# Remainder chunk thresholded by a parametric ReLU on ScalarE, with gMLP jobs, transfers and weight chores in another order

## The chip, the core and the metric

The kernel runs on one core of a Trainium2 chip. The metric is the device time of one execution in microseconds (us). Of the kernel before, three executions took 562.84, 564.09 and 565.11 us; their median is 564.09 us.

## The reference

Thresholded attention over 8 batches of 8 heads (576 positions, 64 dimensions per head) is followed by a gMLP block with a spatial gate. Cut to what matters:

```python
scores = scale * q @ k.T                       # per batch and head, 576 x 576
scores = where(scores >= max(scores) - tau, scores, -1e9)
attn   = exp(scores - max(scores)); attn /= sum(attn)
x      = attn @ v                              # heads side by side: 576 x 512 per batch
h      = relu(x @ w_in); u, v = h[:, :512], h[:, 512:]
v_n    = (v - mean(v)) / sqrt(var(v) + 1e-6)   # over the 512 features of a position
v_s    = w_spatial @ v_n + b_spatial           # over positions, 576 x 576
out    = (u * v_s) @ w_out
```

## The kernel before

**Slots and steps.** Two heads make a pair, and the 32 pairs (four to a batch) are worked through one after another; the time of one pair is a *slot*. A slot has five *steps*, c = 0 to 4, and the running number of a step is g = 5 x slot + c. Steps 0 to 3 take 128 query rows of both heads (a chunk of 128 x 1152 scores). Step 4 is the *remainder chunk*: the last 64 rows of both heads, stacked on 128 partitions (128 x 576).

**What a step does**, in the order in which `step` (L478) writes it into the engines' queues: TensorE multiplies the scores into PSUM (`scores`, L448 and L445); evictions that were held from the step before are done (`held`); the first filler job `f1` runs its products and, if it is of the kind "act", its eviction on ScalarE; VectorE takes the negated row maxima (`negm`, L491); an `f1` of the kind "dve" is evicted on VectorE; ScalarE computes `e = exp(s - max)` (L499); `mask` (L459) runs for the *previous* step's chunk; actions that have become due (`later`) run; and the second filler `f2` runs its products, evicted at once if it is "dve", or in the next step if it is "act". Every engine works its queue off in this order, and so does SyncE's DMA queue (SP), which issues nearly all transfers. [...]

**Mask.** For steps 0 to 3 VectorE computes `p = (e >= exp(-tau)) * e` in bf16 (L464), and after every second step one DMA transpose brings two chunks into `pT` (L468). For the remainder it computes `pr` the same way (L473), and a small transpose makes `ptr` (L476). Because `mask` works for the previous step, `pr` and `ptr` of a slot are written into the queues in step 0 of the next.

**Fillers.** Steps 0 to 2 transpose q and k of the next pair on TensorE (`qk_main`, `qk_rem`); steps 3 and 4 multiply the previous pair's weights by v (`pv`, L266), each ending in a reciprocal `r` (L274) and a product `xn` (L275) on VectorE. When both heads of a pair are done, a DMA transpose writes their part of `xT` (L281). From g = 27 on, each step also has one gMLP job of a finished batch: five `v` jobs (`moe_v`, gate branch), five `u` (`moe_u`), five `s` (`moe_s`, spatial products) and five `o` (`moe_o`, output). The string `ORDER` (L527) sets which job takes which of the batch's 20 steps. If a step has two fillers, those of kind "act" come first.

**The gate branch.** A `v` job's product is evicted by a ReLU with a row sum (`vrel`, L333); POOL makes `nmean` (L335). Through `later.append((1, rest))` one step passes, and then `rest` squares on ScalarE with a row sum (`sq`, L341) and normalizes on POOL in four instructions (L343, L345, L346, L347) into one of the five chunks of `vn`. Every `s` job reads all five chunks (L389).

**Transfers of results.** The transposes into `xT` and the stores of `o` are put into the list `sends`, and `step` issues them after the mask of the same step or, where the eviction came later than that, of the next step. Loads of q, k and v come from a queue that gives up one DMA per step.

**Start, weights, end.** The first loads of q and k go out on two queues (SP and ScalarE's); clearing of buffers is split between POOL (`clear_first`, `clear_rest`) and VectorE; eight transposes of `identf` run on TensorE ahead of the first real ones (L559). The weight *chores* (`load_w_in`, `load_ws`, `shape_ws`, `shape_bias`, `place_bias`, `load_w_o`) hang on certain steps (L519 to L522). After the last scores the list `last` is worked off two jobs at a time; there `moe_v_part` does three quarters of the last batch's `v` products before the last `xT` part has come.

Of the kernel before, what the change touches and what calls it, by code (L numbers as in the profile page):

```python
# [17 lines left out]
def kernel(  # L18
# [38 lines left out]

    identf = const.tile([P, P], F32, name="identf")
    ntau = const.tile([P, 1], F32, name="ntau")
    ctau = const.tile([P, 1], F32, name="ctau")  # L60

    mhalf = const.tile([P, 1], F32, name="mhalf")

    p_ring = [const.tile([P, 2, 1152], BF16, name=f"p{i}") for i in range(2)]
# [3 lines left out]
    ld_ring = [[const.tile([P, 4, 5, D], F32, name=f"{n}{i}") for n in ("ql", "kl", "vl")]  # L68
               for i in range(2)]
    vx_ring = [const.tile([P, 2, D], F32, name=f"vx{i}") for i in range(2)]  # L70
    kd_ring = [const.tile([P, P], F32, name=f"kd{i}") for i in range(2)]
    ptr_ring = [const.tile([P, 5, 192], BF16, name=f"ptr{i}") for i in range(3)]

    def clear_first():
        for t in ld_ring[0][:2]:
            nc.gpsimd.memset(t[64:128, :, 4, :], 0.0)
        nc.gpsimd.memset(kd_ring[0], 0.0)

    def clear_rest():
        nc.gpsimd.memset(ld_ring[0][2][64:128, :, 4, :], 0.0)  # L80
        nc.gpsimd.memset(kd_ring[1], 0.0)
        for t in vx_ring:
            nc.gpsimd.memset(t[0:64], 0.0)
        for t in ld_ring[1]:
            nc.gpsimd.memset(t[64:128, :, 4, :], 0.0)
        for t in v_ring:
            nc.vector.memset(t[:, :, D:D + 1], 1.0)
            nc.vector.memset(t[64:128, 4, D:D + 1], 0.0)
            nc.vector.memset(t[64:128, 9, D:D + 1], 0.0)
            nc.vector.memset(t[0:64, 10, D:D + 1], 0.0)  # L90
        for t in ptr_ring:
            nc.vector.memset(t[:, :, 128:192], 1.0)
        for t in pr_ring:
            nc.vector.memset(t[:, S:640], 0.0)
        for t in vn_ring:
            nc.vector.memset(t[64:128, 4, :], 1.0)

# [5 lines left out]

    def load(i, n, w, eng=nc.sync):

        b, hp = divmod(i, HP)
        t = ld_ring[i // 2 % 2][w][:, 2 * (i % 2):2 * (i % 2) + 2 * n]
        src = (q, k, v)[w][b, 2 * hp:2 * hp + 2 * n]

        def main():  # L110
            eng.dma_start(
                out=t[:, :, 0:4, :],
                in_=src[:, 0:512, :].rearrange("h (p c) d -> p h (c d)", c=4))

        def rest():
            eng.dma_start(out=t[0:64, :, 4, :],
                          in_=src[:, 512:576, :].rearrange("h p d -> p h d"))

        def rest_b():
            nc.sync.dma_start(  # L120
                out=vx_ring[i // 2 % 2][64:128],
                in_=src.rearrange("(j h) s d -> h s j d", h=2)[1, 512:576])
        return [main, rest] + ([rest_b] if w == 2 else [])
# [67 lines left out]
    def shape_bias(_):  # L191
# [6 lines left out]
        nc.gpsimd.tensor_copy(out=parts[:, 2, :], in_=b32)  # L198

    def place_bias(_):  # L200
        for n in range(3):
            nc.sync.dma_start(out=wsT[64 + n:65 + n, 4, 0:S], in_=parts[:, n, :])
# [11 lines left out]
    done_with = set()  # L214
    sends = []
    qks, pts, xns, xts = {}, {}, {}, {}
# [34 lines left out]
    def pv(i, h):  # L251
# [17 lines left out]
        def ev():  # L269
            o = hold["t"][:, 0:325].rearrange("p (c d) -> p c d", d=65)  # L270
            if h == 0:
                xns[i] = xp.tile([P, 5, P], BF16, name="xn")
            r = small.tile([P, 5], F32, name="r")
            nc.vector.reciprocal(out=r, in_=o[:, :, 64])  # L274
            nc.vector.tensor_tensor(out=xns[i][:, :, h * D:(h + 1) * D], in0=o[:, :, 0:64],  # L275
                                    in1=r.unsqueeze(2).broadcast_to([P, 5, 64]), op=ALU.mult)
            if h == 1:
                if hp == 0:
                    xts[b] = xtp.tile([P, 4, 640], BF16, name="xT")
                xn = xns[i]  # L280
                sends.append(lambda: nc.sync.dma_start_transpose(  # L281
                    out=xts[b][:, hp, :].rearrange("p (c s) -> p c s", s=P),
                    in_=xn.rearrange("p c d -> p (c d)")))
        return "dve", mm, ev
# [3 lines left out]

    parted = {}

    def moe_v_part(b, c):

        def mm():
            if c % 3 == 0:
                parted["tile"] = ps_s.tile([P, 1536], F32, name="s")
            t = parted[c] = parted["tile"][:, 512 * (c % 3):512 * (c % 3) + 512]
            for f in range(3):
                nc.tensor.matmul(out=t, lhsT=xts[b][:, f, c * P:(c + 1) * P],
                                 rhs=w_in[:, f, 512:1024], start=(f == 0), stop=False)
        return "act", mm, lambda: None  # L300

    def moe_v(b, c):
        hold = {}

        def mm():
            t = hold["t"] = parted.get(c) if b == B - 1 else bank()
            for f in range(3 if b == B - 1 else 0, 4):
                nc.tensor.matmul(out=t, lhsT=xts[b][:, f, c * P:(c + 1) * P],  # L308
                                 rhs=w_in[:, f, 512:1024], start=(f == 0), stop=(f == 3))
# [101 lines left out]
    def moe_o(b, c):  # L411
# [9 lines left out]
        def ev():  # L421
# [3 lines left out]
            else:  # L425
                nc.scalar.copy(out=o[:n], in_=hold["t"][:n])  # L426
            dst = (out[b, 0:512, :].rearrange("(p c) n -> p c n", c=4)[:, c, :] if c < 4
                   else out[b, 512:576, :])
            sends.append(lambda: nc.sync.dma_start(out=dst, in_=o[:n]))
        return "act", mm, ev  # L430
# [28 lines left out]
    def mask():  # L459
# [11 lines left out]
        else:  # L471
            pt = pr_ring[i % 2]
            nc.vector.scalar_tensor_tensor(out=pt[:, 0:S], in0=e[:, 0, :], scalar=ctau,  # L473
                                           in1=e[:, 0, :], op0=ALU.is_ge, op1=ALU.mult)
            pts[i, 2] = ptr_ring[i % 3]
            nc.sync.dma_start_transpose(out=pts[i, 2][:, :, 0:P], in_=pt)  # L476

    def step(i, c, f1, f2):  # L478
# [17 lines left out]
        if i is not None:  # L496
            e = ep.tile([P, 2, S], F32, name="e")
            for h in range(nh):
                nc.scalar.activation(out=e[:, h, :], in_=s[:, h, :], func=ACT.Exp,  # L499
                                     bias=nm[:, h:h + 1])  # L500
        ready = sends[:]
        sends.clear()
        if unmasked:
            mask()
        for f in ready:
            f()
        if i is not None:
# [10 lines left out]

    chores = {13: (load_bias, 0)}  # L519
    for n, g0, d, f in ((4, 6, 4, load_w_in), (3, 8, 4, load_ws), (5, 23, 3, shape_ws),  # L520
                        (1, 15, 1, shape_bias), (1, 37, 1, place_bias), (2, 42, 5, load_w_o)):
        chores.update({g0 + d * j: (f, j) for j in range(n)})  # L522
# [3 lines left out]
    LAG = 27  # L526
    ORDER = "vuvvuvuvuu" + "oososososs"  # L527
    jobs = {}
    for b in range(B - 1):
        n = dict.fromkeys("vuso", 0)  # L530
        for j, t in enumerate(ORDER):
            f = {"v": moe_v, "u": moe_u, "s": moe_s, "o": moe_o}[t]
            if t != "o" or b:
                jobs[LAG + 20 * b + j] = (f, b - (t == "o"), n[t])
            n[t] += 1
    last = [jobs.pop(g) for g in range(5 * NPAIR, LAG + 20 * B) if g in jobs]
    Z = B - 1
    last += [(moe_o, Z - 1, j) for j in (0, 1)]
    last += [(pv, NPAIR - 1, h) for h in range(2)]
    last += [(moe_v_part, Z, j) for j in range(5)]  # L540
    last += [(moe_v, Z, j) for j in range(5)]
    last += [(moe_o, Z - 1, j) for j in (2, 3, 4)]
    last += [(f, Z, j) for f in (moe_u, moe_s, moe_o) for j in range(5)]
    with tc.manual_schedule():
        for w in (0, 1):
            for f in load(0, 1, w, (nc.sync, nc.scalar)[w]):
                f()
        clear_first()
        make_identity(nc, identf)
        nc.vector.memset(ntau, -float(tau))  # L550
        nc.vector.memset(mhalf, -0.5)
        nc.scalar.activation(out=ctau, in_=ntau, func=ACT.Exp)
        for w in (0, 1):
            for f in load(1, 1, w):
                f()
        for f in load(0, 2, 2):
            f()
        for _ in range(8):
            nc.tensor.transpose(out=ps_f.tile([P, 512], F32, name="f")[:, 0:P], in_=identf,  # L559
                                identity=identf)  # L560
        shape_qk(0)
        for f in (qk_main(0, 0), qk_main(0, 1), qk_rem(0)):
            f[1]()
            f[2]()
        clear_rest()
        shape_qk(1)
        queue = []
        for g in range(5 * NPAIR + (len(last) + 1) // 2):
# [28 lines left out]
        while held:  # L597
            held.pop(0)()
        for f in sends:
            f()  # L600

# [34 lines left out]
```

## Time and profile before

| | |
|---|---|
| Three executions, median | 564.09 us (562.84 to 565.11) |
| The profiled execution's own time | 562.84 us |
| Its span, first to last instruction | 561.1 us |
| TensorE (PE) busy | 487.0 us, 87% |
| VectorE (DVE) busy | 470.5 us, 84% |
| ScalarE (ACT) busy | 328.2 us, 59% |
| GpSimd (POOL) busy | 240.8 us, 43% |
| Mean granted TensorE clock | 0.959 of full speed |

The first negated maximum starts at 12.5 us and the last at 518.6 us, so there are some 12 us of start, 506 us for 32 slots and 43 us of end; a slot takes 15.8 us on average. In the profile a group's line gives line, engine, operation, tiles, shape and count, then busy time, the mean of one in ns, and the idle time of the engine just ahead of it with what ended most of it. A timeline gives start, duration and the instruction; "PE", "DVE", "ACT", "POOL" and "SPq" are TensorE, VectorE, ScalarE, GpSimd and SyncE's DMA queue.

### The profile page before, as it was taken

The numbers are of one execution on the slowest core, as the hardware profiler recorded it, in microseconds if no ns is written. First come the engines' busy times: TensorE is split into PE (matmuls) and PEld (weight loads), VectorE is DVE, ScalarE is ACT, GpSimd is POOL, SyncE is SP. The second block draws the span as 40 slices with busy tenths as digits, with TensorE's granted clock in tenths as the row PEclk, the third lists the DMA queues.
The fourth block names the chain that finished last, engine by engine and source line by source line (L and its number), as shares of the span: only waits on it lengthen the run. The fifth ranks groups of instructions, "written<-read, shape, count | busy, mean of one in ns | idle before, by whom it ended". The sixth has DMA issues, their size and how long they took to land.

```text
span 561.1 us, 10240 instructions
## 1 busy us (share of the span) xinstructions
PE 487.0 (87%) x3848; PEld 257.7 (46%) x3848; DVE 470.5 (84%) x535; ACT 328.2 (59%) x609; POOL 240.8 (43%) x413
## 2 busy tenths in 40 slices
PE   6774887987898999899879999889989999989886
PEld 4342443544354555455435554445444554545433
DVE  3894988997898899889968999889987899989553
ACT  2553454774467755676546765677555766677241
POOL 5426622685407732377204752178303762064020
PEclk9896888997999999999999999999998999999989
DMA  8599797985987888968997698978987588755822
GB/s 235 107 214 185 140 207 134 217 146 125 208 173 158 180 182 184 195 94 224 166 174 145 127 217 150 189 141 165 205 187 157 98 198 188 119 107 102 192 65 84
DMA packets 243601, 90.91 MB, mean 162 GB/s; under 512 B 213024, under 2 KB 238112, under 8 KB 243552
## 3 DMA queue, kind: packets, MB, share of 16 engines
q1 hardware_dynamic: 241936, 88.39, 76.9%
q0 software_dynamic: 1200, 1.58, 2.3%
q8 instruction: 30, 0.49, 0.4%
q10 hardware_dynamic: 416, 0.30, 0.2%
q14 instruction: 19, 0.16, 0.1%
HBM read 33.31 MB, written 9.44 MB: 76 GB/s over the span
## 4 chain that ended last, share of the span: by engine, by line
PE 47%; DVE 24%; DMA 12%; ACT 10%; issue 5%; SPq 1%; POOL 0%; ACTq 0%; POOLq 0%
PE s L445 18%; DVE negm L491 14%; PE f L266 7%; DVE p L464 7%; DMA ptr<-pr 7%; ACT e L499 5%; PE f L389 4%; DMA xT<-xn 4%; PE s L448 3%; PE f L359 3%; PE f L308 3%; PE f L418 3%; ACT sq L341 2%; DVE xn L275 1%; ACT vrel L333 1%
## 5 line engine op out<-in xcount | busy, mean ns | idle before, releaser
L499 ACT ACTIVATE e<-s,negm 128x576 f32<-128x576 f32 x288 | 199.5, 740 | 96.8 <-DVE negm L491 77.4
L491 DVE TENSOR_REDUCE negm<-s 128x2 f32<-128x1152 f32 (+1 forms) x160 | 197.2, 1233 | 47.3 <-PE s L445 45.9
L445 PE MATMUL s<-qkT 64*128 64x512 f32 (+1 forms) x768 | 191.1, 590 | 1.0 <-ACT e L499 1.0
L464 DVE SCALAR_TENSOR_TENSOR p<-e,ctau 128x1152 bf16<-128x1152 f32 x128 | 187.5, 1465 | 0.0
L445 PEld LDWEIGHTS s<-qkT 64*128 64x128 f32 (+1 forms) x768 | 55.6, 173 | 29.2 <-issue 2.8
L247 POOL COPY kd<-qkT 64x64 f32<-64x64 f32 x32 | 13.0, 406 | 129.4 <-ACT qkT L243 124.7
L230 ACT COPY qkT<-f 128x512 f32<-128x512 f32 x64 | 37.6, 588 | 50.1 <-PE f L226 50.1
L266 PEld LDWEIGHTS <-pT 128*128 128x128 bf16 x1280 | 49.1, 100 | 37.4 <-issue 25.8
L448 PE MATMUL s<-kd,qkT 128*128 128x128 f32 x256 | 55.4, 299 | 8.5 <-ACT e L499 5.5
L266 PE MATMUL f<-v,pT 128*128 128x65 bf16 x1260 | 53.1, 197 | 9.0 <-ACT vrel L333 4.6
L448 PEld LDWEIGHTS s<-kd,qkT 128*128 128x128 f32 x256 | 45.5, 197 | 21.8 <-ACT e L499 8.8
L308 PE MATMUL f<-w_in,xT 128*128 128x512 bf16 x140 | 37.8, 387 | 11.0 <-DMA xT<-xn 9.5
L142 POOL COPY kn<-kl 128x640 f32<-128x640 f32 x32 | 26.1, 817 | 32.8 <-DMA kl<-in_k_dram 20.3
L389 PE MATMUL f<-wsT,vn 128*128 128x512 bf16 x150 | 38.0, 384 | 2.1 <-ACT o L426 1.6
L335 POOL TENSOR_SCALAR nmean<-sm 128x1 f32<-128x1 f32 x35 | 11.8, 338 | 64.8 <-ACT vrel L333 64.8
L266 PE MATMUL f<-v,ptr 128*128 128x65 bf16 x315 | 21.2, 199 | 19.2 <-DMA ptr<-pr 19.2
L359 PE MATMUL f<-xT,w_in 128*128 128x512 bf16 x120 | 32.6, 396 | 5.8 <-ACT vrel L333 5.8
L139 POOL TENSOR_SCALAR qn<-ql 128x640 f32<-128x640 f32 x32 | 30.5, 953 | 11.6 <-DMA ql<-in_q_dram 10.7
L418 PE MATMUL f<-w_o,gT 128*128 128x512 bf16 (+1 forms) x128 | 33.8, 388 | 0.5
L333 ACT ACTIVATE vrel<-f 128x512 f32<-128x512 f32 x35 | 20.8, 595 | 20.8 <-PE f L308 20.8
L275 DVE TENSOR_TENSOR xn<-f,r 128x320 bf16<-128x320 f32 x63 | 31.0, 491 | 2.2
L473 DVE SCALAR_TENSOR_TENSOR pr<-e,ctau 128x576 bf16<-128x576 f32 x32 | 31.9, 997 | 0.0
(101 smaller groups left out, 530.5 us busy)
## 6 DMA issues: line engine op xcount, KB each, us to landing
vl<-in_v_dram SPq DMA_DIRECT2D x16, 512.0 KB, 4.7
out_dram<-o SPq DMA_DIRECT2D x32, 256.0 KB, 2.7
ql<-in_q_dram SPq DMA_DIRECT2D x15, 512.0 KB, 4.5
kl<-in_k_dram SPq DMA_DIRECT2D x15, 512.0 KB, 4.6
uT<-in_moe_w_spatial_dram SPq DMA_DIRECT2D x2, 576.0 KB, 5.1
vl<-in_v_dram SPq DMA_DIRECT2D x16, 64.0 KB, 2.8
pT<-p SPq DMA_TRANSPOSE x64, 5.5
w_in<-in_moe_w_in_dram POOLq DMA_DIRECT2D x4, 256.0 KB, 5.7
```

The source lines that it names most:

```text
L230: nc.scalar.copy(out=qks[i][:, which, 0:512], in_=hold["t"])
L266: nc.tensor.matmul(out=t[:, c * 65:c * 65 + 65], lhsT=lhs, rhs=rhs, start=(j == 0), stop=(j == 4))
L275: nc.vector.tensor_tensor(out=xns[i][:, :, h * D:(h + 1) * D], in0=o[:, :, 0:64], in1=r.unsqueeze(2).broadcast_to([P, 5, 64]), op=ALU.mult)
L308: nc.tensor.matmul(out=t, lhsT=xts[b][:, f, c * P:(c + 1) * P], rhs=w_in[:, f, 512:1024], start=(f == 0), stop=(f == 3))
L359: nc.tensor.matmul(out=t, lhsT=w_in[:, m, f * P:(f + 1) * P], rhs=xts[b][:, m, 0:512], start=(m == 0), stop=(m == 3))
L389: nc.tensor.matmul(out=t, lhsT=vn[:, c, f * P:(f + 1) * P], rhs=wsT[:, c, 0:512], start=(c == 0), stop=(c == 4))
L418: nc.tensor.matmul(out=t[:n], lhsT=gs[b][:, f, c * P:c * P + n], rhs=w_o[:, f, :], start=(f == 0), stop=(f == 3))
L445: return nc.tensor.matmul(out=out, lhsT=qk[hs, 0, m], rhs=qk[hs, 1, lo:lo + n], start=True, stop=True)
L448: nc.tensor.matmul(out=view(s, 512, [[448, 2], [1, 64]]), lhsT=qk[:, 0, c * P:(c + 1) * P], rhs=kd_ring[i % 2], start=True, stop=True)
L464: nc.vector.scalar_tensor_tensor(out=pt[:, c % 2, :], in0=ef, scalar=ctau, in1=ef, op0=ALU.is_ge, op1=ALU.mult)
L491: nc.vector.tensor_reduce(out=nm[:, 0:nh], in_=s, axis=AX.X, op=ALU.max, negate=True)
L499: nc.scalar.activation(out=e[:, h, :], in_=s[:, h, :], func=ACT.Exp, bias=nm[:, h:h + 1])
```

## The change

The remainder chunk's threshold moves from VectorE to ScalarE: tau is added to the negated maximum (a 128 x 1 instruction on VectorE), a parametric ReLU with slope 1e30 below zero leaves values at or over the threshold and makes the others hugely negative, and an exp writes straight into `pr` in bf16. All values kept come out larger by exp(tau), which the division by the row sum cancels. Only the transpose into `ptr` stays in `mask`. In the same change the gMLP jobs alternate v, u and then s, o; `sends` is gone, so `xT` transposes and stores are issued where their eviction is written; `moe_v_part` is gone and `last` has another order; the weight chores hang on other steps, and `place_bias` is part of `shape_bias` again; all clearing is done on POOL ahead of the first loads; the first k load goes out on SP; and the eight transposes of `identf` are gone.

```diff
     identf = const.tile([P, P], F32, name="identf")
+    make_identity(nc, identf)
     ntau = const.tile([P, 1], F32, name="ntau")
+    nc.vector.memset(ntau, -float(tau))
...
+    for ts in ld_ring:
+        for t in ts:
+            nc.gpsimd.memset(t[64:128, :, 4, :], 0.0)
+    for t in vx_ring:
+        nc.gpsimd.memset(t[0:64], 0.0)
+    for t in kd_ring:
+        nc.gpsimd.memset(t, 0.0)
+    for t in v_ring:
+        nc.gpsimd.memset(t[:, :, D:D + 1], 1.0)
+        nc.gpsimd.memset(t[64:128, 4, D:D + 1], 0.0)
+        nc.gpsimd.memset(t[64:128, 9, D:D + 1], 0.0)
+        nc.gpsimd.memset(t[0:64, 10, D:D + 1], 0.0)
-    def clear_first():
...
-    def clear_rest():
...
+    for t in ptr_ring:
+        nc.gpsimd.memset(t[:, :, 128:192], 1.0)
+    for t in pr_ring:
+        nc.gpsimd.memset(t[:, S:640], 0.0)
+    for t in vn_ring:
+        nc.gpsimd.memset(t[64:128, 4, :], 1.0)
...
-
-    def place_bias(_):
         for n in range(3):
             nc.sync.dma_start(out=wsT[64 + n:65 + n, 4, 0:S], in_=parts[:, n, :])
...
-                xn = xns[i]
-                sends.append(lambda: nc.sync.dma_start_transpose(
+                nc.sync.dma_start_transpose(
                     out=xts[b][:, hp, :].rearrange("p (c s) -> p c s", s=P),
-                    in_=xn.rearrange("p c d -> p (c d)")))
+                    in_=xns[i].rearrange("p c d -> p (c d)"))
...
-    def moe_v_part(b, c):
...
-            t = hold["t"] = parted.get(c) if b == B - 1 else bank()
-            for f in range(3 if b == B - 1 else 0, 4):
+            t = hold["t"] = bank()
+            for f in range(4):
...
-            sends.append(lambda: nc.sync.dma_start(out=dst, in_=o[:n]))
+            nc.sync.dma_start(out=dst, in_=o[:n])
...
         else:
-            pt = pr_ring[i % 2]
-            nc.vector.scalar_tensor_tensor(out=pt[:, 0:S], in0=e[:, 0, :], scalar=ctau,
-                                           in1=e[:, 0, :], op0=ALU.is_ge, op1=ALU.mult)
             pts[i, 2] = ptr_ring[i % 3]
-            nc.sync.dma_start_transpose(out=pts[i, 2][:, :, 0:P], in_=pt)
+            nc.sync.dma_start_transpose(out=pts[i, 2][:, :, 0:P], in_=pr_ring[i % 2])
...
             e = ep.tile([P, 2, S], F32, name="e")
-            for h in range(nh):
+            if c == 4:
+
+                nc.vector.tensor_scalar_add(out=nm[:, 0:1], in0=nm[:, 0:1], scalar1=float(tau))
+                nc.scalar.activation(out=e[:, 0, :], in_=s[:, 0, :], func=ACT.Prelu,
+                                     bias=nm[:, 0:1], alpha=1e30)
+                nc.scalar.activation(out=pr_ring[i % 2][:, 0:S], in_=e[:, 0, :], func=ACT.Exp)
+            for h in range(2 if c < 4 else 0):
                 nc.scalar.activation(out=e[:, h, :], in_=s[:, h, :], func=ACT.Exp,
                                      bias=nm[:, h:h + 1])
-        ready = sends[:]
-        sends.clear()
         if unmasked:
             mask()
-        for f in ready:
-            f()
...
-    chores = {13: (load_bias, 0)}
-    for n, g0, d, f in ((4, 6, 4, load_w_in), (3, 8, 4, load_ws), (5, 23, 3, shape_ws),
-                        (1, 15, 1, shape_bias), (1, 37, 1, place_bias), (2, 42, 5, load_w_o)):
+    chores = {2: (load_bias, 0)}
+    for n, g0, d, f in ((4, 5, 2, load_w_in), (3, 12, 1, load_ws), (5, 16, 1, shape_ws),
+                        (1, 21, 1, shape_bias), (2, 23, 2, load_w_o)):
         chores.update({g0 + d * j: (f, j) for j in range(n)})
...
     LAG = 27
-    ORDER = "vuvvuvuvuu" + "oososososs"
     jobs = {}
     for b in range(B - 1):
-        n = dict.fromkeys("vuso", 0)
-        for j, t in enumerate(ORDER):
-            f = {"v": moe_v, "u": moe_u, "s": moe_s, "o": moe_o}[t]
-            if t != "o" or b:
-                jobs[LAG + 20 * b + j] = (f, b - (t == "o"), n[t])
-            n[t] += 1
+        for j in range(5):
+            g = LAG + 20 * b + 2 * j
+            jobs[g], jobs[g + 1] = (moe_v, b, j), (moe_u, b, j)
+            jobs[g + 10] = (moe_s, b, j)
+            if b:
+                jobs[g + 11] = (moe_o, b - 1, j)
     last = [jobs.pop(g) for g in range(5 * NPAIR, LAG + 20 * B) if g in jobs]
-    Z = B - 1
-    last += [(moe_o, Z - 1, j) for j in (0, 1)]
-    last += [(pv, NPAIR - 1, h) for h in range(2)]
-    last += [(moe_v_part, Z, j) for j in range(5)]
-    last += [(moe_v, Z, j) for j in range(5)]
-    last += [(moe_o, Z - 1, j) for j in (2, 3, 4)]
-    last += [(f, Z, j) for f in (moe_u, moe_s, moe_o) for j in range(5)]
+    last += [(moe_o, B - 2, j) for j in range(5)]
+    last[6:6] = [(pv, NPAIR - 1, h) for h in range(2)]
+    last += [(f, B - 1, j) for f in (moe_v, moe_u, moe_s, moe_o) for j in range(5)]
     with tc.manual_schedule():
         for w in (0, 1):
-            for f in load(0, 1, w, (nc.sync, nc.scalar)[w]):
+            for f in load(0, 1, w):
                 f()
-        clear_first()
...
-        for _ in range(8):
-            nc.tensor.transpose(out=ps_f.tile([P, 512], F32, name="f")[:, 0:P], in_=identf,
-                                identity=identf)
         shape_qk(0)
         for f in (qk_main(0, 0), qk_main(0, 1), qk_rem(0)):
             f[1]()
             f[2]()
-        clear_rest()
+        for w in (0, 1):
+            for f in load(1, 1, w):
+                f()
         shape_qk(1)
+        for f in load(0, 2, 2):
+            f()
```

More of the change, by code (lines that the diff above doesn't have):

```diff
@@ L58 @@
     identf = const.tile([P, P], F32, name="identf")
+    make_identity(nc, identf)
     ntau = const.tile([P, 1], F32, name="ntau")
+    nc.vector.memset(ntau, -float(tau))
     ctau = const.tile([P, 1], F32, name="ctau")
+    nc.scalar.activation(out=ctau, in_=ntau, func=ACT.Exp)
     mhalf = const.tile([P, 1], F32, name="mhalf")
+    nc.vector.memset(mhalf, -0.5)
     p_ring = [const.tile([P, 2, 1152], BF16, name=f"p{i}") for i in range(2)]
@@ L69 @@
                for i in range(2)]
+    for ts in ld_ring:
+        for t in ts:
+            nc.gpsimd.memset(t[64:128, :, 4, :], 0.0)
     vx_ring = [const.tile([P, 2, D], F32, name=f"vx{i}") for i in range(2)]
+    for t in vx_ring:
+        nc.gpsimd.memset(t[0:64], 0.0)
     kd_ring = [const.tile([P, P], F32, name=f"kd{i}") for i in range(2)]
-    ptr_ring = [const.tile([P, 5, 192], BF16, name=f"ptr{i}") for i in range(3)]
-    def clear_first():
-        for t in ld_ring[0][:2]:
-            nc.gpsimd.memset(t[64:128, :, 4, :], 0.0)
-        nc.gpsimd.memset(kd_ring[0], 0.0)
-    def clear_rest():
[L80 to L96, printed above, removed]
+    for t in kd_ring:
[5 more added lines that the diff above has]
+        nc.gpsimd.memset(t[0:64, 10, D:D + 1], 0.0)
+    ptr_ring = [const.tile([P, 5, 192], BF16, name=f"ptr{i}") for i in range(3)]
+    for t in ptr_ring:
[4 more added lines that the diff above has]
+        nc.gpsimd.memset(t[64:128, 4, :], 1.0)
     w_in = const.tile([P, 4, 1024], BF16, name="w_in")
@@ L101, with load @@
     wsb = const.tile([P, 5, 640], BF16, name="wsb")
-    def load(i, n, w, eng=nc.sync):
+    def load(i, n, w):
         b, hp = divmod(i, HP)
@@ L110, in main @@
         def main():
-            eng.dma_start(
+            nc.sync.dma_start(
                 out=t[:, :, 0:4, :],
@@ L115, in rest @@
         def rest():
-            eng.dma_start(out=t[0:64, :, 4, :],
-                          in_=src[:, 512:576, :].rearrange("h p d -> p h d"))
+            nc.sync.dma_start(out=t[0:64, :, 4, :],
+                              in_=src[:, 512:576, :].rearrange("h p d -> p h d"))
         def rest_b():
@@ L214 @@
     done_with = set()
-    sends = []
     qks, pts, xns, xts = {}, {}, {}, {}
@@ L287 @@
     later = []
-    parted = {}
-    def moe_v_part(b, c):
[L293 to L300, printed above, removed]
     def moe_v(b, c):
@@ L544 @@
+    last = [jobs.pop(g) for g in range(5 * NPAIR, LAG + 20 * B) if g in jobs]
+    last += [(moe_o, B - 2, j) for j in range(5)]
+    last[6:6] = [(pv, NPAIR - 1, h) for h in range(2)]
+    last += [(f, B - 1, j) for f in (moe_v, moe_u, moe_s, moe_o) for j in range(5)]
     with tc.manual_schedule():
         for w in (0, 1):
-            for f in load(0, 1, w, (nc.sync, nc.scalar)[w]):
+            for f in load(0, 1, w):
                 f()
-        clear_first()
-        make_identity(nc, identf)
@@ L550 @@
[L550 to L557, printed above, removed]
-        for _ in range(8):
-            nc.tensor.transpose(out=ps_f.tile([P, 512], F32, name="f")[:, 0:P], in_=identf,
-                                identity=identf)
         shape_qk(0)
@@ L598 @@
             held.pop(0)()
-        for f in sends:
-            f()
 _INS = ['q', 'k', 'v', 'tau', 'moe_w_in', 'moe_w_spatial', 'moe_b_spatial', 'moe_w_out']
```

## The prediction

> **What bounds the kernel now.** I read first the busy shares (section 1), then the 40 slices (section 2), the chain that ended last (section 4) and the costliest groups (section 5).
>
> ```profile
> PE 487.0 (87%) x3848; PEld 257.7 (46%) x3848; DVE 470.5 (84%) x535; ACT 328.2 (59%) x609; POOL 240.8 (43%) x413
> ...
> PE   6774887987898999899879999889989999989886
> DVE  3894988997898899889968999889987899989553
> DMA  8599797985987888968997698978987588755822
> ```
>
> No engine is full by itself: PE and DVE share the bound, and the DMA engines are little behind. I then read the starts of the `negm` instructions, five to a slot, off the DVE timeline. From slot 10 on the slots repeat in fours: 15.8, 15.3, 15.5 us, and then 14.8 to 19.6 us. One of the second kind (slot 11):
>
> ```profile
> 187.18 1.36 DVE L491 TENSOR_REDUCE negm<-s 128x2 f32<-128x1152 f32 x1 [0.40 <-PE s L445]
> 188.45 1.24 DVE L473 SCALAR_TENSOR_TENSOR pr<-e,ctau 128x576 bf16<-128x576 f32 x1
> 189.91 1.36 DVE L491 TENSOR_REDUCE negm<-s 128x2 f32<-128x1152 f32 x1 [0.21 <-PE s L445]
> 191.18 1.41 DVE L464 SCALAR_TENSOR_TENSOR p<-e,ctau 128x1152 bf16<-128x1152 f32 x1
> 193.22 1.36 DVE L491 TENSOR_REDUCE negm<-s 128x2 f32<-128x1152 f32 x1 [0.63 <-PE s L445]
> 194.49 1.58 DVE L464 SCALAR_TENSOR_TENSOR p<-e,ctau 128x1152 bf16<-128x1152 f32 x1
> 195.99 1.34 DVE L491 TENSOR_REDUCE negm<-s 128x2 f32<-128x1152 f32 x1
> ```
>
> The reader is to see that ahead of steps 0, 1 and 2 DVE waited for scores (PE ended last), ahead of step 3 for nothing; and that `pr` (L473) lies in a step where DVE waited anyway. The long fourth slots come from the transfer queue:
>
> ```profile
> 284.04 0.56 SPq L429 DMA_DIRECT2D out_dram<-o  x1
> 284.69 0.55 SPq L111 DMA_DIRECT2D ql<-in_q_dram  x1
> 285.34 1.24 SPq L476 DMA_TRANSPOSE ptr<-pr  x1
> 286.63 2.85 SPq L281 DMA_TRANSPOSE xT<-xn  x1
> ...
> 292.19 0.39 PE L308 MATMUL f<-w_in,xT 128*128 128x512 bf16 x1 [3.36 <-DMA xT<-xn]
> ```
>
> The batch's last `xT` part stands behind a store, a load and `ptr`; PE idles 3.36 us for it.
>
> **What the Trainium skill says.** "ScalarE: Activation LUTs", *What ACT_TABLE_LOAD costs*: a change of table set costs a 1283 ns load and a drain, and an activation with a pointer bias about 280 ns + 0.833 ns per element, whatever the function. For 576 elements that is an estimate of 760 ns; the trace has 740 for the exp, and one table load of 1283 ns. The compiled program of the changed kernel still has one table load, so the parametric ReLU shares the exp's set. "TensorE: Matmul & The Clock Gate", *What's actually happening*: after an idle window of about 3.4 us the clock falls to half. The trace agrees in kind: after the idle 3.36 us above, the next four score products took 1.61 us instead of 1.13, four `u` products 1.89 instead of 1.04. "SBUF — State Buffer", *Who interferes with whom*: DVE instructions in 2-port modes or with two SBUF inputs hold up GpSimd's reads. In the trace the same POOL instruction (L346) takes 0.19 us alone and 600 ns in the mean; I take the short values where DVE idles.
>
> **Part 1: remainder on ScalarE.** Removed from DVE: 32 x 997 ns = 31.9 us (L473). Added: 32 small adds; nearest row L323, a DVE 128x1 TENSOR_SCALAR of 154 ns, so 4.9 us. DVE gets 27 us less. ACT gets 32 x 0.74 = 23.7 us more and stays near 60%; in step 0 its next exp waits for `negm`, and that gap covers it. Where `pv` is f1 in step 4, the add stands behind `r` and `xn`, which starts the parametric ReLU some 1 to 2 us later; the next exp waits for a later `negm` anyway. DVE relief reaches the end only in step 0 where DVE is not waiting for PE: about 0.5 us in the third and fourth kind of slot, less elsewhere. `ptr` comes earlier only if SP is free; it is not (its transposes follow one another above). I take -4 us; bounds -15 (half of DVE's relief) and +3.
>
> **Part 2: job order.** Now the fifth `v` takes job step 8 and is evicted in step 9; its `rest` is due in step 10, and the first `s` is written in that same step, straight after it. Before they were five job steps apart. `s` reads the fifth `vn` chunk, so PE waits, with the next step's scores queued behind, and behind those `negm`, the exps and the mask. The chain, from rows for one chunk that DVE hardly disturbed:
>
> ```profile
> 233.50 0.72 ACT L341 ACTIVATE sq<-vrel,nmean 128x512 bf16<-128x512 f32 x1
> 234.12 0.20 ACT L341 ACTIVATION_READ_ACCUMULATOR sq<-vrel,nmean 128x1 f32 x1
> 234.40 0.19 POOL L343 TENSOR_SCALAR rs<-ss 128x1 f32<-128x1 f32 x1 [0.59 <-ACT sq L341]
> 234.67 0.55 POOL L345 TENSOR_TENSOR rs<-rs,mhalf 128x1 f32<-128x1 f32 x1
> 235.30 0.19 POOL L346 TENSOR_TENSOR nm<-nmean,rs 128x1 f32<-128x1 f32 x1
> 235.60 0.77 POOL L347 TENSOR_SCALAR vn<-vrel,rs,nm 128x512 bf16<-128x512 f32 x1
> ```
>
> From the start of `negm` in step 2 of slot 11 (193.22): `negm` and two exps end at 195.98 (2.76 us), `sq` with its read-out ends 0.92 later, POOL ends 2.05 after that: 5.75 us. Then the fifth product (0.39) and the next scores (0.47 + 1.13), which overlap a little: `negm` of step 3 starts 7.7 us after that of step 2, against 2.77 before: 4.9 us lost. PE idles about 4 us (it has two transposes and four products meanwhile), long enough for half clock. The 0.5 + 0.85 us of the example, with the next transposes and `pv` partly covered, say 1.2. Seven batches stand in the loop (slots 7 to 31): 7 x 6.1 = +43 us. Bounds: 3.5 per batch (+25), if part of it takes the place of existing waits, and 8 (+56), if POOL is disturbed or the half clock lasts longer.
>
> **Part 3: `sends` gone.** In step 4 of the third kind of slot `pv` is f2, so its `xT` transpose waited for the next step. Now it is issued right after that step's `pT`, ahead of store, load and `ptr` (284.04 instead of 286.63: 2.6 us). The excess of the fourth-kind slots over 14.8 and of the third over 15.5 sums to some 12 us between slots 13 and 25; I take 10 as gone. Slot 7 (19.2 us) waits 3.8 us for `ptr`, which falls into the new wait: -4. Late next is `ptr`, 1.3 us behind `xT`, but with over two steps to spare. Stores now stand ahead of `pT`, on an ACT copy that ends before the mask: 0. Together -14 (bounds -18, 0).
>
> **Part 4: chores.** The same instructions, crowded: five `shape_ws` in consecutive steps (POOL 1.10 + 1.09 us each), then five bias instructions of 5.7 us, and three DMAs on SP that wait for them with `pT` behind. POOL needs about 20 us in steps that last 17. Weight loads crowd into slots 1 and 2, where the DMA share already is 0.91. +3 (bounds -3, +8).
>
> **Part 5: start.** POOL clears everything first: eight f32 blocks near 0.25 us apart, three `ptr` blocks of 0.37 (row L167), two `vn` blocks of 0.5 (DVE row L96), sixteen small ones of 0.1: the first `qn` starts near 7.4 us instead of 5.42. k on SP comes 1.3 us later, within that. Without the eight transposes the first products may stay at half clock a little longer: +0.5. Sum +2.5 (bounds +1, +5).
>
> **Part 6: end.** The `v` products no longer start ahead of the last `xT`, but six `o` jobs (about 0.86 us each) lie there instead: 0 (bounds -4, +3).
>
> **Sum.** 562.84 (the profiled execution's own time: span 561.1 and 1.7 around it) - 4 + 43 - 14 + 3 + 2.5 + 0 = 593 us. The median of the runs is 1.2 higher, within the range.
>
> **Rivals.**
> 1. *Covered wait.* The `vn` wait costs 3.5 us per batch, SP and DMA catch up in it, and the clock stays: 562.8 + 25 - 16 - 4 + 5 = 573. For it: the DMA share is 0.85 in the middle; against it: PE and DVE are in order and nothing behind the wait can run early.
> 2. *VectorE decides (the other side).* DVE's 27 us come off in full, in step 0 of each slot, and `pr` on ScalarE shortens the `ptr` path (7% of the chain). With a wait of 3.5 us: 562.8 - 27 + 25 - 14 + 5 = 552. It turns the sign if the wait costs under (27 + 14 - 5.5)/7 = 5.1 us per batch. For it: DVE at 84%, "DMA ptr<-pr 7%" in the chain. Against: DVE waits for PE ahead of the steps concerned.
> 3. *Crowded start.* Chores and weight loads stall slots 2 to 5 by more than 8 us: about 605. The early slots, at 0.91 DMA share, speak for it; that the bytes are the same speaks against it.
> 4. *Table loads at each change of function*: 64 x 1.28 = +82 us; the program's single load excludes it.
>
> **How the numbers follow.** The main case (582 to 602) gets 0.66, rival 1 (565.5 to 582) 0.17, rival 2 0.07, rival 3 and worse 0.07; 0.03 is left for sums that cancel. Main case and rival 1 share the forecast's side. The range 570 to 607 leaves out rival 2 and the outer ends. About 0.5%, 2.8 us, can be told from no change: faster 0.07, same 0.04, slower 0.89.
>
> **What would show it.** Right: PE idle of about 4 us ahead of one `vn` weight load per batch, released by POOL (the normalization that is L347 before), some 28 us in all; step 2 of slots 7, 11, 15 ... near 7.5 us; a half-clock stretch after it; fourth-kind slots under 15.5 us and the wait for `xT` mostly gone; first `negm` near 15 us; DVE near 443 us busy, ACT near 352. Wrong: step 2 of these slots under 5 us, or step 0 shortened by 0.8 us in every slot.

## The result: 2.8% slower, and the profile after

The changed kernel took 580.5 us (median of 579.23 to 581.24); the kernel before, run beside it, 564.6 us. The ratio is 1.0278, with a 95% interval of 1.0237 to 1.0319. All ratios here leave disturbed executions out, so a ratio can differ a little from that of two medians. The profiled execution has a span of 579.4 us, 18.3 more than before. Lines of the page that answer to those shown of before:

```profile
PE 495.8 (86%) x3840; PEld 259.5 (45%) x3840; DVE 442.7 (76%) x512; ACT 349.9 (60%) x641; POOL 230.7 (40%) x436
...
PE   3885784996989799996999889996999979998896
DVE  0996793985998769886898869985998959987443
DMA  7699998979488886978698765978699666655732
```

VectorE has 27.8 us less work and ScalarE 21.7 more, as the change says; neither number shows in the time. In the groups a new wait has come up, ahead of the spatial products (columns as before: busy, mean of one, idle before and what ended it):

```profile
L370 PE MATMUL f<-wsT,vn 128*128 128x512 bf16 x150 | 39.7, 387 | 29.9 <-POOL vn L328 28.6
```

It is seven waits of at most 4.4 us. One of them, in slot 11, in the TensorE timeline and then in POOL's:

```profile
196.89 1.13 PE L426 MATMUL s<-qkT 64*128 64x512 f32 x4
197.95 0.33 PE L234 MATMUL f<-identf,qn 128*128 128x128 f32 x1
198.12 0.27 PE L234 MATMUL f<-identf,kn 128*128 128x128 f32 x1
198.36 1.02 PE L370 MATMUL f<-wsT,vn 128*128 128x512 bf16 x4
203.77 0.61 PE L370 MATMUL f<-wsT,vn 128*128 128x512 bf16 x1 [4.38 <-POOL vn L328]
204.16 0.63 PE L429 MATMUL s<-kd,qkT 128*128 128x128 f32 x2
204.73 2.08 PE L426 MATMUL s<-qkT 64*128 64x512 f32 x4
```

```profile
201.75 0.19 POOL L324 TENSOR_SCALAR rs<-ss 128x1 f32<-128x1 f32 x1 [2.47 <-ACT sq L322]
202.02 0.55 POOL L326 TENSOR_TENSOR rs<-rs,mhalf 128x1 f32<-128x1 f32 x1
202.65 0.19 POOL L327 TENSOR_TENSOR nm<-nmean,rs 128x1 f32<-128x1 f32 x1
202.95 0.76 POOL L328 TENSOR_SCALAR vn<-vrel,rs,nm 64x512 bf16<-64x512 f32 x1
```

Four spatial products run, the fifth waits for POOL's last instruction, and the scores of the next step stand behind it and then run at half pace: 2.08 us for four products instead of 1.13. `negm` of step 2 started at 198.07 and that of step 3 at 206.85; so step 2 takes 8.8 us where it took 2.8. It takes 8.8 us in each of slots 7, 11, ... 27, and 5.6 us in slot 31. The transfer queue shows the second large effect, in the stretch that was shown of before:

```profile
295.11 2.69 SPq L449 DMA_TRANSPOSE pT<-p  x1
297.89 1.24 SPq L275 DMA_TRANSPOSE xT<-xn  x1
299.23 0.53 SPq L109 DMA_DIRECT2D ql<-in_q_dram  x1
299.85 1.58 SPq L454 DMA_TRANSPOSE ptr<-pr  x1
```

The `xT` transpose now goes out straight behind `pT`, ahead of the load and of `ptr`. TensorE's weight loads wait 0.5 us for `xT` in all, where they waited 12.4 (before and after; us and times):

```profile
  PEld L308: 12.4, 7
```

```profile
  PEld L289: 0.5, 1
```

Read off the starts of `negm`, the slots stand so (us; slots 10 to 29):

| slots | before | after | job order alone | direct issue alone |
|---|---|---|---|---|
| 10, 14, ... | 15.8 | 15.0 | 14.9 | 15.8 |
| 11, 15, ... | 15.3 | 20.7 to 22.0 | 20.9 to 22.0 | 15.3 |
| 12, 16, ... | 15.5 to 16.5 | 15.6 | 15.5 | 15.5 to 15.8 |
| 13, 17, ... | 14.8 to 19.6 | 14.0 to 14.3 | 14.7 to 18.4 | 14.4 to 14.6 |

That slots 15 and 27 take 22.0 us after the change and slots 11 and 23 only 20.7 is not the wait, which is 4.38 us in all four. TensorE's mean granted clock was 0.92 of full speed in slot 11 and 0.84 in slot 15: there the half pace lasted longer.

### The profile page after: what moved, and what is told of

Same layout as the page of the kernel before. It is cut to its first block, busy times and chain, and to the rows that moved or that the text cites. A ratio compares the mean times of both kernels' runs of the same rounds, so it can differ in the third digit from the quotient of the medians.

```text
span 579.4 us, 10244 instructions
## 1 busy us (share of the span) xinstructions
PE 495.8 (86%) x3840; PEld 259.5 (45%) x3840; DVE 442.7 (76%) x512; ACT 349.9 (60%) x641; POOL 230.7 (40%) x436
## 4 chain that ended last, share of the span: by engine, by line
PE 41%; DVE 30%; issue 8%; ACT 7%; DMA 7%; POOL 4%; SPq 1%; POOLq 0%; ACTq 0%; DVEq 0%
PE s L426 17%; DVE p L445 13%; DVE negm L469 12%; PE f L261 5%; ACT e L483 4%; PE f L289 4%; PE s L429 4%; DMA ptr<-pr 3%; PE f L399 2%; PE f L370 2%; PE f L340 2%; DMA pT<-p 2%; PE f L221 2%; DVE xn L270 2%; ACT sq L322 2%
## 5 line engine op out<-in xcount | busy, mean ns | idle before, releaser
L426 PE MATMUL s<-qkT 64*128 64x512 f32 (+1 forms) x768 | 196.5, 604 | 1.0 <-ACT e L483 1.0
L370 PE MATMUL f<-wsT,vn 128*128 128x512 bf16 x150 | 39.7, 387 | 29.9 <-POOL vn L328 28.6
L429 PE MATMUL s<-kd,qkT 128*128 128x128 f32 x256 | 58.0, 311 | 7.7 <-ACT e L483 5.6
L407 ACT COPY o<-f 128x512 f32<-128x512 f32 (+1 forms) x32 | 18.6, 582 | 54.0 <-PE f L399 52.0
L225 ACT COPY qkT<-f 128x512 f32<-128x512 f32 x64 | 37.6, 588 | 22.0 <-PE f L221 20.7
L479 ACT ACTIVATE e<-s,negm 128x576 f32<-128x576 f32 x32 | 23.6, 737 | 44.6 <-DVE negm L478 44.6
L140 POOL COPY kn<-kl 128x640 f32<-128x640 f32 x32 | 31.1, 972 | 27.2 <-DMA kl<-in_k_dram 22.1
L384 DVE TENSOR_TENSOR gT<-f,uT 128x512 bf16<-128x512 f32 x30 | 20.6, 686 | 26.4 <-PE f L370 19.0
L316 POOL TENSOR_SCALAR nmean<-sm 128x1 f32<-128x1 f32 x35 | 16.5, 472 | 53.4 <-ACT vrel L314 52.6
L370 PEld LDWEIGHTS <-vn 128*128 128x128 bf16 x160 | 14.8, 97 | 50.1 <-POOL vn L328 32.0
L399 PE MATMUL f<-w_o,gT 128*128 128x512 bf16 (+1 forms) x128 | 37.1, 417 | 0.0
L340 PE MATMUL f<-xT,w_in 128*128 128x512 bf16 x120 | 30.9, 380 | 0.0
```

What stands on the lines that cost most here:

```text
L225: nc.scalar.copy(out=qks[i][:, which, 0:512], in_=hold["t"])
L340: nc.tensor.matmul(out=t, lhsT=w_in[:, m, f * P:(f + 1) * P], rhs=xts[b][:, m, 0:512], start=(m == 0), stop=(m == 3))
L370: nc.tensor.matmul(out=t, lhsT=vn[:, c, f * P:(f + 1) * P], rhs=wsT[:, c, 0:512], start=(c == 0), stop=(c == 4))
L399: nc.tensor.matmul(out=t[:n], lhsT=gs[b][:, f, c * P:c * P + n], rhs=w_o[:, f, :], start=(f == 0), stop=(f == 3))
L426: return nc.tensor.matmul(out=out, lhsT=qk[hs, 0, m], rhs=qk[hs, 1, lo:lo + n], start=True, stop=True)
L429: nc.tensor.matmul(out=view(s, 512, [[448, 2], [1, 64]]), lhsT=qk[:, 0, c * P:(c + 1) * P], rhs=kd_ring[i % 2], start=True, stop=True)
```

## Experiments: one part of the change at a time

Every kernel was timed beside the kernel before. First the parts done alone on the kernel before.

**The job order** (`before_new_order`):

```diff
-    ORDER = "vuvvuvuvuu" + "oososososs"
+    ORDER = "vuvuvuvuvu" + "sososososo"
```

> The kernel before with the gMLP jobs in the changed kernel's order, v and u in turn and then s and o in turn, nothing else of the change. Theory (vn wait of 6 us in seven batches, less what it saves in other waits, some 10 us): 564 + 43 - 10 = 597 us, step 2 of every fourth slot at 8.8 us or more. Rival (the wait is absorbed): under 580 us.

Measured: 592.84 us, ratio 1.0576 (1.0525 to 1.0626), some 32 us. From the list of waits:

```profile
PE f L389 <- POOL vn L347: 24.3, 6, 4.4
PE f L266 <- DMA ptr<-pr: 12.4, 5, 5.9
PE f L308 <- DMA xT<-xn: 9.7, 5, 2.5
```

The order alone makes the wait for `vn`, and more than the whole loss of the change. (Six waits are listed here; that of slot 7, 6.7 us, the list puts down to the instruction that follows the normalization on POOL.) The waits for `xT` stay at 9.7 us (9.5 before): the transfer queue does not catch up in the `vn` wait. A gain that nobody had priced is in the table: slots 10, 14, ... are 0.9 us shorter with v and u in turn.

**Direct issue** (`before_direct`; both calls of `sends.append` become plain calls, and, as one half of it, `before_direct_xt` with the first alone):

```diff
-                sends.append(lambda: nc.sync.dma_start_transpose(
+                nc.sync.dma_start_transpose(
...
-            sends.append(lambda: nc.sync.dma_start(out=dst, in_=o[:n]))
+            nc.sync.dma_start(out=dst, in_=o[:n])
```

> The kernel before with the transposes into xT and the stores issued where their eviction is written, nothing else of the change. Theory (the transposes into xT come 2.6 us earlier, and the waits for them in the fourth-kind slots go): about 12 us less, 552 us, no PE wait for xT over 1 us. Rival (in the changed kernel these waits went because the transfer queue catches up in the vn wait): 560 us or more, the waits for xT stay at 5 us or more in all.

> The kernel before with only the transposes into xT issued where they are written; the stores keep their delayed issue. Theory (the gain of direct issue is the earlier xT): 543 us within 2, as with both. Rival (the stores' place matters as well, since a store held back stands ahead of ptr and xT): some 550 us, half the gain.

Measured: both calls together 542.88 us, ratio 0.968 (0.964 to 0.972); the transposes alone 542.83 us, 0.9704 (0.9659 to 0.9749). More than expected, 18 us, and all of it from the transposes; the stores' place makes no difference that the intervals show. TensorE's weight loads wait 0.8 us for `xT` (1.4 with the transposes alone) where they waited 12.4. The queue of the first of the two:

```profile
276.40 2.73 SPq L467 DMA_TRANSPOSE pT<-p  x1
279.23 1.25 SPq L280 DMA_TRANSPOSE xT<-xn  x1
280.57 0.54 SPq L111 DMA_DIRECT2D ql<-in_q_dram  x1
281.21 1.41 SPq L475 DMA_TRANSPOSE ptr<-pr  x1
```

From issue to landing `xT` has a median of 2.6 us here against 3.4 before: it is not only issued earlier, it also lands sooner. A likely reason, not tried alone, is that the 512 KB load now stands behind it and not ahead.

**The remainder chunk on ScalarE** (`before_prelu`; the change's edits in `mask` and `step` that concern `Prelu` and `pr_ring`):

> The kernel before with the remainder chunk on ScalarE and nothing else of the change. Theory A (the prediction's): VectorE is relieved of 27 us, of which 4 us reach the end: 560 us. Theory B (read from the trace after, where undisturbed slots are 0.7 to 1.1 us shorter): 0.6 us in each of 32 slots, 545 us. Theory C: ScalarE's second pass delays the next step: above 565 us.

Measured: 560.9 us, ratio 0.9997 (0.9968 to 1.0026): no difference. Step 0 of slot 10 in the DVE timeline shows why:

```profile
171.12 1.36 DVE L488 TENSOR_REDUCE negm<-s 128x2 f32<-128x1152 f32 x1 [0.21 <-PE s L445]
173.85 1.36 DVE L488 TENSOR_REDUCE negm<-s 128x2 f32<-128x1152 f32 x1 [1.37 <-PE s L445]
```

The mask is gone from between the two maxima, and VectorE waits for TensorE instead: the step still takes 2.73 us. In the whole execution VectorE's idle time that ended with scores grew, from the first line (before) to the second (us in total, times, longest):

```profile
DVE negm L491 <- PE s L445: 45.9, 66, 8.1
```

```profile
DVE negm L488 <- PE s L445: 66.0, 71, 8.0
```

Most of the relief turned into idle time. Theory B, which I had read from shorter slots in the trace after, falls: those slots are shorter by the job order and by direct issue.

**The chores** (`before_chores`; the two lines of `chores`, and `place_bias` inside `shape_bias`):

> The kernel before with the weight chores on the changed kernel's steps (place_bias again inside shape_bias), nothing else of the change. Theory (read from the trace after: slot 4 takes 23.1 us instead of 15.3, because three small DMAs stand on SP and wait for POOL, with ptr and pT around them): 4 to 8 us more, 566 to 570 us, slot 4 over 20 us. Rival (the long slot 4 only takes the place of waits in slots 2, 3 and 7): within 2 us of the kernel before.

Measured: 560.43 us, ratio 1.0028 (0.9994 to 1.0063). The expectation of 4 us and more fails. Slot 4 does take 22.0 us, but slots 2 and 7 take 13.4 and 15.3 instead of 21.9 and 19.2; slots 0 to 9 together take 159.5 us against 158.9. The crowd moves a stall from one early slot to another.

**The start** (`before_start`; the change's hunks ahead of `queue = []` and those for clearing):

> The kernel before with the changed kernel's start (all clearing on POOL ahead of everything, first k load on SP, no eight transposes of identf), nothing else of the change. Theory (the first negm of the changed kernel starts 1.95 us later): first negm at 14.4 us, 2 us more in all. Rival (the transfers that the start overlaps with bound the first slots anyway, so the delay is swallowed by slot 2): under 0.5 us.

Measured: 563.61 us, ratio 1.0057 (1.0032 to 1.0082), 3.2 us: later slots do not swallow it.

Then the changed kernel with its wait altered.

**The spatial job one step later** (`after_swap`):

```diff
-            jobs[g + 10] = (moe_s, b, j)
+            jobs[g + 11] = (moe_s, b, j)
             if b:
-                jobs[g + 11] = (moe_o, b - 1, j)
+                jobs[g + 10] = (moe_o, b - 1, j)
```

> The changed kernel with one thing altered: in the second half of each batch's twenty job steps the output job comes first and the spatial job second, so every spatial job sits one step later. Theory (the wait for the fifth vn chunk costs some 6 us in each of seven batches): PE reaches the chunk about 1 us before POOL has it instead of 4.4 us, step 2 of slots 11, 15, ... falls from 8.8 to about 3 us, no half-clock stretch follows, and the kernel takes about 580 - 7 x 5 = 545 us. Rival (the wait only stands where waits for transfers would stand otherwise): the fourth-kind slots grow back from 14.0 to over 16 us, and the time falls by 10 us or less, to 570.

Measured: 558.96 us, ratio to the kernel before 0.9956 (0.993 to 0.9981). Against the changed kernel (1.0278) some 18 us are won: the rival's 10 is too little, but the theory's 35 too much. In slots 11, 15, ... step 2 fell from 8.8 to 2.6 us as expected, but step 3 now takes 5.8 to 7.1 us, against 3.2 to 4.3 in the changed kernel. What is left of the wait, in slot 11, from the timeline of all engines:

```profile
197.76 0.55 POOL L326 TENSOR_TENSOR rs<-rs,mhalf 128x1 f32<-128x1 f32 x1
...
198.34 1.41 DVE L445 SCALAR_TENSOR_TENSOR p<-e,ctau 128x1152 bf16<-128x1152 f32 x1
198.39 1.41 POOL L327 TENSOR_TENSOR nm<-nmean,rs 128x1 f32<-128x1 f32 x1
199.90 0.77 POOL L328 TENSOR_SCALAR vn<-vrel,rs,nm 64x512 bf16<-64x512 f32 x1
...
200.73 0.61 PE L370 MATMUL f<-wsT,vn 128*128 128x512 bf16 x1 [1.85 <-POOL vn L328]
...
201.26 2.19 PE L426 MATMUL s<-qkT 64*64 64x288 f32 x8
```

In the changed kernel the stalled VectorE left POOL alone, and `nm` took 0.19 us. Here VectorE keeps running, its mask starts just ahead of `nm`, and `nm` takes 1.41 us, as long as the mask. That agrees with the rule of the Trainium skill ("SBUF — State Buffer", *Who interferes with whom*) by which a VectorE instruction with two inputs in SBUF holds up a POOL instruction that reads SBUF. After the idle stretch of 1.85 us the next products ran at half pace: 2.19 us for eight that take 1.19 otherwise. The length of the stretch does not settle that. It is the same in slot 15, from TensorE's timeline:

```profile
264.13 0.39 PE L370 MATMUL f<-wsT,vn 128*128 128x512 bf16 x1 [1.85 <-POOL vn L328]
264.45 1.19 PE L426 MATMUL s<-qkT 64*64 64x288 f32 x8
```

Here they ran at full pace, and the half pace came about 1.5 us later (granted clock 0.50 from 266 to 269 us). After stretches of 1.85 to 1.86 us the eight products took 2.19, 1.19, 2.19, 2.18 and 1.34 us in slots 11, 15, 19, 23 and 27, and 1.19 after 2.46 us in slot 7.

**The old job order** (`after_old_order`; the loop over `ORDER` put back):

> The changed kernel with the job order of the kernel before, all else as changed. Theory (the order alone cost the kernel before some 31 us, and moving the spatial job by one step gave back only 21 because POOL's chain runs into VectorE's mask): no wait for a vn chunk is left, 580 - 31 = 549 us. Rival (direct issue already saves the same waits, so the two do not add up): 558 us or more, as with the spatial job one step later.

Measured: 548.69 us, ratio 0.98 (0.9758 to 0.9841), as the theory said: the two large parts add up.

**TensorE kept at work in the wait** (`after_warm`):

```diff
             t = hold["t"] = bank()
+            if f == 0 and b < B - 1:
+                for _ in range(34):
+                    nc.tensor.transpose(out=t[:, 0:P], in_=identf, identity=identf)
```

> The changed kernel with 34 transposes of identf ahead of the first spatial job of each of the seven batches in the loop, into the bank that this job then overwrites: TensorE has 34 x 0.11 = 3.7 us of work in the stretch in which it waits for the vn chunk, and nothing else is altered. Theory (part of the loss, 1.2 us a batch, is the half clock after the idle stretch): step 2 of slots 11, 15, ... falls from 8.8 to about 7.7 us, and the time by 7 x 1.2 = 8 us, to 572. Rival (the half clock costs nothing, since TensorE is not waited for right after): 580 us.

Measured: 568.08 us, ratio to the kernel before 1.0161 (1.0122 to 1.0199) against the changed kernel's 1.0278: 1.2% less (0.4 to 2.0 by the ends of the two intervals), by work that computes nothing. By slots, the five of the kind 11, 15, ... give 10 us in the two traces, of which the one of the changed kernel is from the slowest of its four executions. In slot 11:

```profile
196.15 3.93 PE L370 MATMUL f<-identf 128*128 128x128 f32 x34
200.14 0.81 PE L373 MATMUL f<-wsT,vn 128*128 128x512 bf16 x3
201.55 0.39 PE L373 MATMUL f<-wsT,vn 128*128 128x512 bf16 x1 [0.61 <-POOL vn L328]
201.78 0.38 PE L432 MATMUL s<-kd,qkT 128*128 128x128 f32 x2
202.09 1.13 PE L429 MATMUL s<-qkT 64*128 64x512 f32 x4
```

Step 2 falls from 8.8 to 7.4 us, and slots 11, 15, ... from 21.3 in the mean to 19.3. So the half pace had cost 2.0 us in such a slot, 1.4 of them in step 2. The wait itself costs 4.6, the difference between step 2's 7.4 and the 2.8 of the kernel before. The other steps together are 0.6 shorter than before, which makes a net loss of some 6.1 us. In slot 31, where TensorE had waited for only 2.3 us, the transposes last longer than the wait: step 2 grows from 5.6 to 6.6 us.

**Better than both.** Direct issue with v and u in turn, but the spatial jobs left where they were (`before_direct_alt`), and with the remainder chunk on ScalarE as a trial:

```diff
-    ORDER = "vuvvuvuvuu" + "oososososs"
+    ORDER = "vuvuvuvuvu" + "oososososs"
```

> The kernel before with transposes and stores issued where they are written, and v and u jobs in turn in the first half of the twenty steps (the second half stays oososososs, so the first spatial job is four steps after the last v). Theory (slots 10, 14, ... take 14.9 us with v and u in turn against 15.8 with vuvvuvuvuu): 0.9 us in each of six or seven slots less than direct issue alone, 543 - 6 = 537 us. Rival (the time comes back in the next slot, where one more v stands): 543 us.

> The kernel before with transposes and stores issued where they are written, and the remainder chunk on ScalarE. Theory A (the parametric ReLU is worth nothing, because TensorE and not VectorE is waited for in the steps that it relieves): as direct issue alone, 543 us within 2. Theory B (with the waits for xT gone VectorE is nearer to the bound, so its 27 us count): 535 us or less.

> The kernel before with direct issue, v and u in turn ahead of oososososs, and the remainder chunk on ScalarE: what the runs so far speak for, together. If the parametric ReLU adds nothing: 537 us, as without it. If it counts once the waits are gone: 533 us or less.

Measured: 537.07 us, ratio 0.9598 (0.9547 to 0.9649), for `before_direct_alt`. With the remainder on ScalarE, direct issue has 0.9635 (0.9589 to 0.968) against 0.968 without it, and the full combination 0.9597 (0.9529 to 0.9665) against 0.9598. The intervals of each pair overlap, and direct issue with the parametric ReLU takes 540.5 us, so theory B (535 us or less) has no support. `before_direct_alt` is the best of these kernels that changes least: two edits, 4% under the kernel before. Its lead over direct issue alone (0.968) is less sure, since the ends of these two intervals still overlap. The expected 537 us were hit partly by luck. Slots 10, 14, ... do take 14.9 us, but slots 11, 15, ... take 15.7 instead of 15.3, so that nearly half of the 0.9 us comes back, as the rival said; some 2.6 us of the gain lie in slots 0 to 9.

## Why the prediction was right, and where its terms were off

The time lies within the range, on the side that was forecast, and the wait that was named causes the loss. But the sum said +30 us and the change costs 16. The measured 580.5 us lie just below the main case's own window (582 to 602) and in that of rival 1 (565.5 to 582): the range holds them only because it took in that rival. By parts, with the ratios above turned to us at some 560:

| part | predicted | alone, measured |
|---|---|---|
| remainder on ScalarE | -4 | 0 (-2 to +1) |
| job order | +43 | +32 |
| `sends` gone | -14 | -18 |
| chores | +3 | +1.6 (0 to +4) |
| start | +2.5 | +3.2 |
| end | 0 | +0.2 (traces: 42.5 and 42.6 us after the start of the last `negm`) |

The measured ratios multiply to 1.032, against 1.0278 for the change as a whole; the difference is within their intervals.

*The wait.* The chain was right almost to the digit: POOL's end was put 5.75 us after the start of `negm` and came 5.64 after it (198.07 to 203.71). The 4.9 us for the wait were near the 4.6 that `after_warm` shows, the 1.2 for the half pace too little against 2.0. The half clock was read from one example, slot 17, and only its next products were counted. That the loss per batch, 6.1 us, is exactly the mean loss of slots 11, 15, ... is luck: the loss also holds the 0.6 us by which the other steps got shorter, mostly step 1 (3.3 to 2.8 us, in the trace of the order alone too), and nobody had priced them.

*The term that was mis-sized* is the step from one batch to seven. It took 6.1 for all of them, with slot 7's old wait subtracted in another part. In the trace of the order alone slot 7 loses 4.2 us and slot 31, the last one, 3.1. And part 2 left out, without a reason, that v and u in turn shorten slots 10, 14, ... by 0.9 us in six or seven places, some 5 us. The job order's +43 should have read about +32. Why that alternation is quicker was not tried.

*`sends`.* Right in kind and place; -10 for the fourth-kind slots was too small. They lost all of their excess and more: even the shortest of them, 14.8 us, went to 14.4, and the sum over the five slots fell by 14 us. The excess itself was added up wrongly: from the same starts it is 13.9 us, not some 12. The step "I take 10 as gone" also counted only the earlier issue and not that `xT` lands sooner after it.

*VectorE.* That relief reaches the end only where VectorE is not waiting for TensorE was the right reason, and -4 was still too generous. Rival 2 fails on its decisive point: the relief is worth 0 and not 27 us alone, and nothing clear with the waits for `xT` gone. Rival 1 (a wait of 3.5 us a batch) comes nearest to the total, but for another reason than it gave: the wait was long, and other slots gave back. Rival 3 fails: the early slots trade stalls among themselves. Rival 4 is excluded: the trace after has one table load of 1283 ns, and the parametric ReLU takes 737 ns (L479), the exp 740.

*Signs named ahead.* Right: 28.6 us of PE idle released by POOL ("some 28"), VectorE at 442.7 and ScalarE at 349.9, fourth-kind slots under 15.5, no wait for `xT`. The step was put near 7.5 us and took 8.8, because of the slower products; without them, in `after_warm`, it took 7.4.

## What to carry to other kernels

An in-order queue makes the distance between a producer's last instruction and its consumer a size to be budgeted: add up the chain between them at the durations it has *while the other engines run*, and leave at least that many steps. Before work is moved off a busy engine, look at what ended its idle time in the very step that is relieved: if another engine ended last there, the relief turns into waiting. And with one queue for transfers, the order of issue is part of the schedule: a small transfer that the next product waits for should go out ahead of large ones that nobody needs yet.

## What the hardware did that was not expected

In the trace after, six stretches of 4.4 us without work on TensorE were each followed by products at half pace (2.08 instead of 1.13 us for four). A stretch need not be that long, nor reach the window of about 3.4 us that the prediction goes by: after 1.85 us the next products ran at half pace in three slots of `after_swap`, and at full or nearly full pace in two. What decides between them stays open. And 34 transposes per batch that compute nothing took 1.2% off the time. The cost of a wait on TensorE is thus not its length alone: here 2.0 us came on top of 4.6.
